# Taking weight signs from ScalarE to VectorE and a magnitude from VectorE to ScalarE, under a new set of order ranks

## The chip, the core and the metric

The kernel runs on one core of a Trainium2 chip. Its time is the device time of that core in microseconds (us), as the median of three runs. The engines are TensorE (PE, matmuls; its weight loads run beside them as PEld), VectorE (DVE), ScalarE (ACT), GpSimd (POOL), and the DMA queue that SyncE (SP) issues.

## What is computed

Three stages follow each other, with 4 x 576 = 2304 tokens of width 512 between them:

```python
scores = where(mask_local or mask_strided, q @ k.T / 8, -1e9)   # 4 batches, 8 heads, 576 tokens, 64 wide
x = softmax(scores) @ v                                         # 2304 x 512
h = x @ w_in;  g = maximum(0.01 * h, h);  x = g @ w_out         # layer 1, 512 -> 2048 -> 512
h = x @ w_in;  g = maximum(h, 0) + log1p(exp(-abs(h)))          # layer 2, its own weights
return g @ w_out
```

The four weight matrices arrive as 64-bit floats, the rest as 32-bit floats.

## The kernel before, in words

**Precision.** Every operand of the big products is split into two 16-bit floats, a high part and a rest, and a product is three matmuls (`mm3`, L461 to L464: high x high, high x rest, rest x high). `project` (L466) makes one block of h in 12 matmuls.

**Preparing a weight quarter.** A weight matrix is handled in four quarters of 2 MB (class `Weight`, from L140). `load` (L147) is a DMA on SP's queue. `largest` (L156, DVE) takes the biggest magnitude. `low` (L162, DVE) shifts the lower 32-bit word of each 64-bit number right by 29. `scale` (from L166, small DVE instructions) makes a scaling factor from the largest, after a matmul on PE (L122) has spread it over all partitions. `shift` (L209, ACT) multiplies the upper words, read as 32-bit floats, by that factor. `merge` (L214, DVE) shifts the upper word left by 3 and ORs the lower word in, which makes a 32-bit float; the left shift loses the sign, so the sign has to stand in the top bit of the lower word before that. There are two ways to put it there:

- `sign` (L198, DVE): takes the top 16 bits of the upper word AND 0x8000 and writes them into the top 16 bits of the lower word. It needs only the loaded word. Layer 2's two matrices use it.
- `sign_of_scaled` (L205, ACT): copies the scaled upper word as a 16-bit float into the same place; what is left of so small a number is its sign. It needs `shift` first. Layer 1's two matrices use it.

Then `high` (L221, ACT) and `rest` (L226, on POOL for layer 1's first matrix, on DVE for layer 2's first) or `rest_of` (L230, DVE) make the two 16-bit parts. `plan_quarter` (L730 on) plans this for layer 1's w_in (W1, four separate quarters) and layer 2's w_in (W2); `plan_together` (L695 on) plans layer 1's w_out (O1), all four quarters under one common scale. The chains are: W1 and O1: load, largest and low, scale, shift, sign of scaled, merge, high, rest. The areas that O1 is loaded into are those that W1's quarters leave, so each of O1's loads waits for a rest of W1.

**Stages.** First the attention of batches 0 and 1 runs beside the preparation of W1 and O1. Layer 1 is cut into eight units of 288 tokens: eight steps of `gate1` (PE, then L483 and L486 on ACT, L489 on POOL) and 16 blocks of the second product. Batches 2 and 3 and the preparation of layer 2's weights run beside layer 1. Layer 2 is cut into nine units of 256 tokens with eight steps each, 72 in all.

**A step of layer 2** (class `Unit`): `first` (PE, 24 matmuls into one of two h buffers in PSUM); `size` (L1136, DVE) clears the sign bits of h and writes |h| to SBUF; `relu` (L1143, ACT) writes max(h, 0) scaled, and frees the h buffer; `soft` (L1150 and L1151, ACT) makes ln(1 + exp(-scale x |h|)); `add` (L1155, POOL); `sums` (L1163, four DVE instructions); `cut_high` (L1167, ACT); `cut_rest` (L1171, DVE); `second` (PE, 21 matmuls). The results of `relu` have two places, and the place of step k is freed by `cut_rest` of step k for step k + 2.

**What sets the order.** Every operation is given to a `Plan` with an engine, a cost in us, what it depends on and a rank. `Plan.run` (L551 on) plays the schedule through in the costs given and issues the operations in that order: of those on an engine that could start within 0.5 us of the earliest, the one with the lowest rank is issued first. `RANKS` (L40) gives each kind of operation a start value and a slope. Engines run their instructions in the order issued. While PE would wait in the first 130 us of this schedule, dummy matmuls (L92) are put in. The plan books `sign_of_scaled` at 1.9 us, `sign` at 2.35 and `size` at 0.6.

Of the kernel before, what the change touches and what calls it, by code (L numbers as in the profile page):

```python
# [10 lines left out]
F16 = mybir.dt.float16  # L11
F32 = mybir.dt.float32
I32 = mybir.dt.int32
U32 = mybir.dt.uint32
U16 = mybir.dt.uint16
AF = mybir.ActivationFunctionType
ALU = mybir.AluOpType
# [4 lines left out]
B, H, S, D = 4, 8, 576, 64  # L22
# [17 lines left out]
RANKS = {  # L40
# [10 lines left out]
}  # L51
# [4 lines left out]
def build(tc, qt, kl, ks, v, wi1, wo1, wi2, wo2, mloc, mstr, out):  # L56
    nc = tc.nc
    with ExitStack() as ctx:
# [82 lines left out]
        class Weight:  # L141
# [54 lines left out]
            def sign(self, q):  # L196
# [3 lines left out]
                )  # L200

            def sign_of_scaled(self, q):

                w = self.t[q].bitcast(F16).rearrange("p s (n t) -> p s n t", t=4)
                nc.scalar.activation(w[:, :, :, 1], self.words(q)[1].bitcast(F32), AF.Copy)  # L205

# [380 lines left out]
        W1, O1, W2, O2 = Weight("i1", wi1), Weight("o1", wo1), Weight("i2", wi2), Weight("o2", wo2)  # L587
# [26 lines left out]
        plan = Plan({"mm": 2, "sc": 1, "pt": 1, "po": 1, "s": 4, "a": 3, "t": 3, "qk": 5, "rs": 2, "x2": 2, "gr": RING, "ob": 2}, idle, 130.0)  # L614
# [85 lines left out]
        def plan_together(W, name, after, parts, then, w1):  # L700
# [6 lines left out]
            for q in range(4):  # L707
                ld = plan.add("SP", 5.9, lambda q=q: W.load(q, area(q)), after[q], ("L" + name, q))
                big = step("DVE", 2.2, lambda q=q: W.largest(q, m()[:, q : q + 1]), [ld], q)
                low = step("DVE", 1.14, lambda q=q: W.low(q), [ld], q + 0.1, port=True)  # L710
                loads.append(big)
                read.append([big, low])

# [14 lines left out]
            for q in range(4):  # L728
                y = step("ACT", 2.07, lambda q=q: W.shift(q, st["s"]), [t] + read[q], 4 + q)
                y = step("ACT", 1.9, lambda q=q: W.sign_of_scaled(q), [y], 4 + q)  # L730
                y = step("DVE", 2.2, lambda q=q: W.merge(q), [y], 4 + q, port=True)
                y = step("ACT", 1.85, lambda q=q: W.high(q, parts(q), O1.by[:, q : q + 1]), [y] + made[-1:] * (q % 2), 4 + q)
                made.append(
                    step("DVE", 2.3, lambda q=q: W.rest_of(q, O1.by[:, q : q + 1]), [y], 4 + q, port=True)
                )
            return made, scaled

        def plan_quarter(W, name, q, place, after, parts, after_read, then=None, eng="DVE"):
# [21 lines left out]
            y = step("DVE", 1.14, lambda: W.low(q), [ld], 0.1, port=True)  # L760
            if not then:
                y = step("DVE", 2.35, lambda: W.sign(q), [y], 0.2, port=True)
            y = step("ACT", 2.07, lambda: W.shift(q, st["s"]), [sc, x, y], 0.3)
            if then:
                y = step("ACT", 1.9, lambda: W.sign_of_scaled(q), [y], 0.3)
            y = step("DVE", 2.2, lambda: W.merge(q), [y], 0.4, port=True)
# [131 lines left out]
        A, A1 = at[0], at[1]  # L898
# [174 lines left out]
        class Unit:  # L1073
# [34 lines left out]
            def scales(self):  # L1108
                new = lambda n, t: sml.tile([P, n], F32, name=t, tag=t)
                self.sc, self.nsc = new(4, "x2s"), new(4, "x2n")  # L1110
                nc.vector.tensor_scalar(
                    out=self.sc, in0=late["u2"], scalar1=self.p2, scalar2=2.0 ** -14, op0=ALU.mult, op1=ALU.mult
                )
                nc.vector.tensor_scalar(out=self.nsc, in0=self.sc, scalar1=-1.0, scalar2=None, op0=ALU.mult)

# [18 lines left out]
            def size(self, k):  # L1134
                t = self.a[k] = tmp.tile([P, 2, U1], F32, name="t", tag="t")[:, :, :U2]
                nc.vector.tensor_scalar(  # L1136
                    out=t.bitcast(I32), in0=self.ps[k].bitcast(I32), scalar1=0x7FFFFFFF, scalar2=None, op0=ALU.bitwise_and
                )

# [8 lines left out]
            def soft(self, k):  # L1148
                a = self.a[k]
                nc.scalar.activation(a, a, AF.Exp, scale=self.nsc[:, k // 2 : k // 2 + 1])  # L1150
                nc.scalar.activation(a, a, AF.Ln, bias=1.0)  # L1151
# [75 lines left out]
        for u in range(NU2):  # L1227
# [9 lines left out]
            for k in range(NK):  # L1237
# [4 lines left out]
                )  # L1242
                size = plan.add("DVE", 0.6, bind(U.size), [g1], rank("Fd", k), take=["t"])
                relu = plan.add(
# [95 lines left out]
```

## Time and profile before

| what | value |
|---|---|
| median of three runs | 870.89 us (870.03 to 873.74) |
| the profiled execution's own time | 871.47 us |
| its span | 869.5 us |
| mean granted TensorE clock in it | 0.995 |
| PE busy, of the span | 831.9 us, 96% |
| DVE busy | 533.7 us, 61% |
| ACT busy | 528.3 us, 61% |
| POOL busy | 265.0 us, 30% |

The shares are averages over stages with different limits. A busy PE says that matmuls were in the engine, dummy ones among them, and not that it was at its peak. The table by stretches (below) tells the stages apart.

### The profile page before, as it was taken

What the parts mean: (1) busy time and instruction counts of PE and PEld (TensorE: products, weight loads), DVE (VectorE), ACT (ScalarE), POOL (GpSimd) and SP (SyncE); (2) the same over time, 40 slices, a digit from 0 to 9 for tenths busy, and PEclk for the clock granted to TensorE, in tenths of its full rate; (3) what the DMA queues carried; (4) which work ended last, traced back from release to release, by engine and by line L of the source; (5) the groups of instructions that cost most, each with busy time, mean ns of one, the idle gap of its engine ahead of it and who ended that gap; (6) DMA issues with size and microseconds to landing.
All of it is one profiled execution on the core that took longest, in us unless ns stands there. A gap on an engine that the chain in (4) does not pass through costs nothing.

```text
span 869.5 us, 17639 instructions
## 1 busy us (share of the span) xinstructions
PE 831.9 (96%) x7330; PEld 684.6 (79%) x7330; DVE 533.7 (61%) x1232; ACT 528.3 (61%) x938; POOL 265.0 (30%) x194
## 2 busy tenths in 40 slices
PE   9888798799999999999999999999999999999997
PEld 5556576578777777787777777888888888888886
DVE  4895652542033535049647859977787778677684
ACT  5899979933456542263726457757575666657572
POOL 2365753120332124140504124323222322223131
PEclk9999999999999999999999999999999999999999
DMA  8932320121013470013221120000000000000000
GB/s 329 390 126 112 140 98 1 67 81 56 1 58 138 158 304 25 2 41 154 98 97 29 71 98 1 26 2 25 2 25 2 25 2 26 1 26 1 26 25 25
DMA packets 10991, 63.27 MB, mean 73 GB/s; under 512 B 1344, under 2 KB 1440, under 8 KB 7840
## 3 DMA queue, kind: packets, MB, share of 16 engines
q1 hardware_dynamic: 10656, 62.00, 19.0%
q8 instruction: 57, 0.93, 0.4%
q10 hardware_dynamic: 256, 0.16, 0.1%
q14 instruction: 22, 0.18, 0.1%
HBM read 57.44 MB, written 4.72 MB: 71 GB/s over the span
## 4 chain that ended last, share of the span: by engine, by line
PE 69%; ACT 12%; DVE 11%; DMA 3%; issue 3%; POOL 1%; SPq 0%; DVEq 0%; ACTq 0%; POOLq 0%
PE h L462 11%; PE h L464 11%; PE h L463 11%; PE o L462 10%; PE o L464 10%; PE o L463 10%; ACT pair L205 3%; ACT pair L209 2%; DMA pair<-wo_dram 2%; ACT s L368 2%; PE ps L322 2%; DVE pair L1005 2%; PE po L419 2%; PE pt L399 1%; ACT t L483 1%
## 5 line engine op out<-in xcount | busy, mean ns | idle before, releaser
L462 PE MATMUL h<-x,w 128*128 128x256 f16 (+1 forms) x1088 | 303.5, 279 | 7.2 <-ACT t L483 5.0
L464 PE MATMUL h<-x,w 128*128 128x256 f16 (+1 forms) x1088 | 303.4, 279 | 4.3 <-POOL w L226 4.3
L463 PE MATMUL h<-x,w 128*128 128x256 f16 (+1 forms) x1088 | 303.4, 279 | 0.0
L1155 POOL TENSOR_TENSOR pair<-pair,t 128x512 f32<-128x512 f32 x72 | 100.4, 1394 | 268.6 <-ACT t L1151 171.1
L489 POOL TENSOR_TENSOR g<-t,g 128x576 f16<-128x576 f32 x64 | 104.3, 1633 | 183.7 <-ACT g L486 181.7
L462 PE MATMUL o<-g,pair 128*128 128x288 f16 x512 | 147.7, 288 | 2.8 <-ACT pair L221 1.8
L464 PE MATMUL o<-g,pair 128*128 128x288 f16 x512 | 147.6, 288 | 2.5 <-DVE pair L230 2.5
L463 PE MATMUL o<-g,pair 128*128 128x288 f16 x512 | 147.5, 288 | 0.0
L463 PEld LDWEIGHTS <-w 128*128 128x128 f16 x1088 | 106.5, 98 | 27.3 <-issue 8.7
L464 PEld LDWEIGHTS <-w 128*128 128x128 f16 x1088 | 106.4, 98 | 24.3 <-POOL w L226 5.2
L462 PEld LDWEIGHTS <-w 128*128 128x128 f16 x1088 | 106.4, 98 | 19.4 <-issue 0.2
L1167 ACT ACTIVATE gr<-pair,x2b 128x896 f16<-128x896 f32 x72 | 74.0, 1038 | 57.2 <-DVE pair L1163 57.2
L1171 DVE SCALAR_TENSOR_TENSOR gr<-pair,x2b,gr 128x896 f16<-128x896 f32 x72 | 86.4, 1209 | 24.8 <-ACT gr L1167 24.7
L1163 DVE TENSOR_TENSOR pair<-pair 128x128 f32<-128x128 f32 x288 | 80.2, 324 | 16.8 <-POOL pair L1155 14.3
L1143 ACT ACTIVATE pair<-h,x2s 128x512 f32<-128x512 f32 x72 | 49.0, 680 | 60.0 <-DVE t L1136 54.4
L464 PE MATMUL o<-w,gr 128*128 128x256 f16 x306 | 83.4, 273 | 0.9 <-DVE gr L1171 0.7
L462 PE MATMUL o<-w,gr 128*128 128x256 f16 x306 | 83.4, 273 | 0.0
L463 PE MATMUL o<-w,gr 128*128 128x256 f16 x306 | 83.4, 273 | 0.0
L390 POOL TENSOR_TENSOR s<-s,sm 96x512 f32<-96x512 f32 (+3 forms) x48 | 43.7, 931 | 121.4 <-DVE sm L385 64.1
L483 ACT ACTIVATE t<-h,gs 128x576 f32<-128x576 f32 x64 | 47.0, 735 | 49.0 <-PE h L464 48.8
L1136 DVE TENSOR_SCALAR t<-h 128x512 int32<-128x512 int32 x72 | 48.7, 685 | 29.0 <-PE h L464 28.4
L214 DVE SCALAR_TENSOR_TENSOR pair<-pair 128x2048 int32<-128x2048 int32 x16 | 37.4, 2338 | 45.9 <-ACT pair L205 35.3
(123 smaller groups left out, 1391.1 us busy)
## 6 DMA issues: line engine op xcount, KB each, us to landing
pair<-wo_dram SPq DMA_DIRECT2D x12, 2048.0 KB, 7.8
pair<-wi_dram SPq DMA_DIRECT2D x8, 2048.0 KB, 10.1
out_dram<-pair SPq DMA_DIRECT2D x18, 256.0 KB, 2.2
q<-qt_dram SPq DMA_DIRECT2D x12, 288.0 KB, 5.9
v<-v_dram SPq DMA_DIRECT2D x2, 1408.0 KB, 7.7
pair<-v_dram SPq DMA_DIRECT2D x2, 1408.0 KB, 6.0
k<-ks_dram SPq DMA_DIRECT2D x7, 288.0 KB, 3.3
k<-kl_dram SPq DMA_DIRECT2D x5, 304.0 KB, 3.8
```

Of the source, the lines that this page charges most:

```text
L390: nc.gpsimd.tensor_tensor(out=sv, in0=sv, in1=rs, op=ALU.mult)
L462: nc.tensor.matmul(ps, ah, bh, start=first, stop=False)
L463: nc.tensor.matmul(ps, ah, bl, start=False, stop=False)
L464: nc.tensor.matmul(ps, al, bh, start=False, stop=last)
L483: nc.scalar.activation(t, ps, AF.Prelu, scale=gates[f // 4], alpha=0.01)
L489: nc.gpsimd.tensor_tensor(out=g[:, 1, f : f + 2, :], in0=t, in1=g[:, 0, f : f + 2, :], op=ALU.subtract)
L1136: nc.vector.tensor_scalar(out=t.bitcast(I32), in0=self.ps[k].bitcast(I32), scalar1=0x7FFFFFFF, scalar2=None, op0=ALU.bitwise_and)
L1143: nc.scalar.activation(r[:, :4].rearrange("p (j h) n -> p j (h n)", j=2), self.ps[k], AF.Relu, scale=self.sc[:, k // 2 : k // 2 + 1],)
L1155: nc.gpsimd.tensor_tensor(out=r, in0=r, in1=self.a[k], op=ALU.add)
L1163: nc.vector.tensor_tensor(out=r[:, o], in0=r[:, x], in1=r[:, y], op=op)
L1167: nc.scalar.activation(self.a[k][:, 0], self.r[k][:, 1:], AF.Copy, scale=self.ag)
L1171: nc.vector.scalar_tensor_tensor(out=a[:, 1], in0=self.r[k][:, 1:], scalar=self.ag, in1=a[:, 0], op0=ALU.mult, op1=ALU.subtract)
```

## The change

Layer 1's weights take their sign with `sign` on DVE, ahead of `shift`; `sign_of_scaled` is gone. For O1's fourth quarter the sign is ranked behind the common scale's first step. `size` becomes one ACT instruction, Prelu with slope -1 below zero and the scale of the column block, which gives the scaled magnitude; it now also waits for the unit's scales; Exp takes the constant -1 as its scale; the small DVE instruction that negated the scales is gone. All values of `RANKS` are new (36 pairs; the first rows and some others are shown).

```diff
-    "A0": (904.756, 0.733), "A1": (1181.967, 5.007), "A2": (1400.517, 32.745), "A3": (-265.753, 0.202),
-    "B0": (380.721, 6.480), "B1": (387.831, 20.804), "B2": (1471.672, 0.086), "B3": (530.207, 2.562),
...
-    "Fp": (-127.497, 0.075), "G0": (-198.498, 0.175), "G1": (1158.664, 0.271), "G2": (688.143, 68.364),
...
-    "O2l": (1380.929, 1.863), "S": (1139.158, 120.000), "S0": (1133.607, 120.000), "S1": (1442.075, 3.830),
-    "S2": (1500.000, 39.240), "W1m": (975.007, 5.818), "W1r": (1347.663, 2.158), "W2": (753.358, 37.166),
+    "A0": (840.876, 58.763), "A1": (1228.229, 40.415), "A2": (1416.066, 23.406), "A3": (497.717, 1.948),
+    "B0": (986.082, 6.642), "B1": (23.082, 0.143), "B2": (-175.176, 0.166), "B3": (496.207, 3.176),
...
+    "Fp": (-256.548, 21.319), "G0": (127.840, 0.080), "G1": (938.559, 22.340), "G2": (1155.015, 12.177),
...
+    "O2l": (1245.704, 0.744), "S": (867.671, 120.000), "S0": (882.390, 0.657), "S1": (1330.594, 0.312),
+    "S2": (1391.819, 36.045), "W1m": (350.471, 14.309), "W1r": (1476.384, 24.622), "W2": (-240.922, 1.069),
...
-            def sign_of_scaled(self, q):
-
-                w = self.t[q].bitcast(F16).rearrange("p s (n t) -> p s n t", t=4)
-                nc.scalar.activation(w[:, :, :, 1], self.words(q)[1].bitcast(F32), AF.Copy)
...
                 low = step("DVE", 1.14, lambda q=q: W.low(q), [ld], q + 0.1, port=True)
+                sign = step("DVE", 2.35, lambda q=q: W.sign(q), [low], q + 0.2 + 0.86 * (q == 3), port=True)
                 loads.append(big)
-                read.append([big, low])
+                read.append([big, sign])
...
                 y = step("ACT", 2.07, lambda q=q: W.shift(q, st["s"]), [t] + read[q], 4 + q)
-                y = step("ACT", 1.9, lambda q=q: W.sign_of_scaled(q), [y], 4 + q)
...
-            if not then:
-                y = step("DVE", 2.35, lambda: W.sign(q), [y], 0.2, port=True)
+            y = step("DVE", 2.35, lambda: W.sign(q), [y], 0.2, port=True)
             y = step("ACT", 2.07, lambda: W.shift(q, st["s"]), [sc, x, y], 0.3)
-            if then:
-                y = step("ACT", 1.9, lambda: W.sign_of_scaled(q), [y], 0.3)
...
-                self.sc, self.nsc = new(4, "x2s"), new(4, "x2n")
+                self.sc = new(4, "x2s")
...
-                nc.vector.tensor_scalar(out=self.nsc, in0=self.sc, scalar1=-1.0, scalar2=None, op0=ALU.mult)
...
-                nc.vector.tensor_scalar(
-                    out=t.bitcast(I32), in0=self.ps[k].bitcast(I32), scalar1=0x7FFFFFFF, scalar2=None, op0=ALU.bitwise_and
-                )
+                nc.scalar.activation(t, self.ps[k], AF.Prelu, scale=self.sc[:, k // 2 : k // 2 + 1], alpha=-1.0)
...
-                nc.scalar.activation(a, a, AF.Exp, scale=self.nsc[:, k // 2 : k // 2 + 1])
+                nc.scalar.activation(a, a, AF.Exp, scale=-1.0)
...
-                size = plan.add("DVE", 0.6, bind(U.size), [g1], rank("Fd", k), take=["t"])
+                size = plan.add("ACT", 0.6, bind(U.size), [g1, scaled], rank("Fa", k), take=["t"])
```

## Rows read from the trace of the kernel before

**Rows 1.** Busy time by stretch: stretch, length, PE, PEld, DVE, ACT, POOL, PEclk, DMA share, GB/s
```profile
22.00:51.00 29.00, 24.23 (x211) 15.02 (x210) 24.69 (x72) 24.74 (x78) 8.71 (x9) 1.00 0.73 301
51.00:130.00 79.00, 67.62 (x613) 52.41 (x612) 51.70 (x157) 70.79 (x137) 52.92 (x32) 1.00 0.35 127
130.00:172.00 42.00, 34.25 (x280) 26.25 (x277) 17.54 (x26) 40.29 (x35) 10.34 (x6) 0.99 0.10 35
172.00:178.00 6.00, 5.38 (x24) 3.44 (x25) 5.97 (x5) 6.00 (x22) 0.00 (x0) 0.52 0.00 0
178.00:500.00 322.00, 320.54 (x2779) 255.59 (x2777) 147.25 (x341) 149.00 (x309) 87.88 (x66) 1.00 0.24 89
500.00:560.00 60.00, 56.05 (x501) 48.43 (x500) 49.62 (x81) 37.95 (x50) 19.92 (x11) 1.00 0.10 38
560.00:862.00 302.00, 302.00 (x2768) 270.83 (x2767) 223.41 (x526) 187.70 (x260) 80.45 (x62) 1.00 0.04 15
```

**Rows 2.** The same view for the dummy matmuls of L92 alone, PE
```profile
22.00:51.00 29.00, 10.27 (x43) 1.00 0.73 301
51.00:180.00 129.00, 1.15 (x3) 0.97 0.26 92
```

**Rows 3.** Groups by line, ACT: busy us, mean ns of one, idle before and releaser
```profile
L205 ACT ACTIVATE pair<-pair 128x2048 f16<-128x2048 f32 x8 | 38.3, 4784 | 0.1
L1143 ACT ACTIVATE pair<-h,x2s 128x512 f32<-128x512 f32 x72 | 49.0, 680 | 60.0 <-DVE t L1136 54.4 <-DVE gr L1171 4.7
L483 ACT ACTIVATE t<-h,gs 128x576 f32<-128x576 f32 x64 | 47.0, 735 | 49.0 <-PE h L464 48.8 <-POOL s L390 0.2
L78 ACT ACT_TABLE_LOAD x1 | 1.3, 1283 | 0.7 <-PEq L1330 0.7
```

**Rows 4.** Timelines of ACT, DVE, POOL and PE: W1's first quarter up to its first product
```profile
39.88 4.77 ACT L205 ACTIVATE pair<-pair 128x2048 f16<-128x2048 f32 x1
44.68 2.29 DVE L214 SCALAR_TENSOR_TENSOR pair<-pair 128x2048 int32<-128x2048 int32 x1 [2.90 <-ACT pair L205]
49.09 4.08 POOL L226 TENSOR_TENSOR w<-pair,w 128x2048 f16<-128x2048 f32 x1 [10.13 <-ACT w L221]
53.22 0.30 PE L464 MATMUL h<-x,w 128*128 128x288 f16 x1 [1.54 <-POOL w L226]
```

**Rows 5.** The chain that ended last, at the end of O1's preparation: start, us
```profile
163.19 4.80 ACT pair L205
168.01 2.29 DVE pair L214
...
172.62 0.42 PE o L464
```

**Rows 6.** Groups by line, DVE, and line L198 alone (ns min/median/max, first and last start)
```profile
L1136 DVE TENSOR_SCALAR t<-h 128x512 int32<-128x512 int32 x72 | 48.7, 685 | 29.0 <-PE h L464 28.4
...
L198 DVE TENSOR_SCALAR pair<-pair x8: 2458/2466/3441, 328.9 to 520.0; 128x2048 uint16<-128x2048 uint16 x8
```

**Rows 7.** Timeline of DVE: the first merge of O1, and DVE's idle time before it
```profile
138.88 2.29 DVE L214 SCALAR_TENSOR_TENSOR pair<-pair 128x2048 int32<-128x2048 int32 x1 [8.72 <-ACT pair L205]
```

**Rows 8.** Timelines of POOL and DVE: an add alone, and one begun beside a sign
```profile
513.68 1.27 POOL L1155 TENSOR_TENSOR pair<-pair,t 128x512 f32<-128x512 f32 x1 [3.75 <-ACT t L1151]
520.01 3.44 POOL L1155 TENSOR_TENSOR pair<-pair,t 128x512 f32<-128x512 f32 x1 [1.99 <-ACT pair L1143]
520.00 2.47 DVE L198 TENSOR_SCALAR pair<-pair 128x2048 uint16<-128x2048 uint16 x1
```

**Rows 9.** Timelines of ACT and DVE: one turn of relu's two places in layer 2
```profile
665.05 0.69 ACT L1143 ACTIVATE pair<-h,x2s 128x512 f32<-128x512 f32 x1 [6.29 <-DVE t L1136]
670.58 1.28 DVE L1171 SCALAR_TENSOR_TENSOR gr<-pair,x2b,gr 128x896 f16<-128x896 f32 x1 [0.39 <-ACT gr L1167]
671.96 0.69 ACT L1143 ACTIVATE pair<-h,x2s 128x512 f32<-128x512 f32 x1
```

10 rows, old and new, of the table RANKS are left out of this document.

## The prediction

> **What bounds the kernel now.** I read the busy time by stretch first, because the averages of the page mix stages. From 178 us on PE has work nearly without a gap: 320.5 of 322 us, then all of 302 us from 560 to 862 [rows 1]. There the other engines are covered, and time can be won only where PE stands still. It stands still in two places. One is the front. Between 51 and 130 us PE is idle for 11.4 us (79 less 67.6), between 130 and 172 for 7.8, and between 172 and 178 for 0.6. In that last stretch the granted clock is 0.52, the lower of its two levels (1.2 GHz of 2.4), after 42 us with the 7.8 us of gaps: 24 matmuls took 5.38 us, 0.224 each, where one takes 320.5 / 2779 = 0.115 later on. That is 2.6 us more [rows 1]. Dummy matmuls hide another 10.3 us of waiting from 22 to 51 us, and 1.2 after [rows 2]. The other place is the start of layer 2, 500 to 560 us: PE idle for 3.95 us, while DVE is busy for 49.6 of 60 [rows 1].
>
> Who holds PE up in the front is seen in the ACT column: 70.8 of 79 us, then 40.3 of 42, then 6.0 of 6 [rows 1]. Second I read the groups of ACT. The sign of the scaled word costs 4.78 us an instruction, eight times, 38.3 us in all [rows 3]; the plan that fixed the order books it at 1.9. Third I followed it along the chains. In W1's first quarter it runs from 39.9 to 44.7, DVE's merge waits for it, then come the high part, POOL's rest and PE's first full product at 53.2 [rows 4]. At the end of O1 the chain of waits goes sign, merge, rest, product: 163.2 to 172.6 us [rows 5]. DVE meanwhile sits idle for 8.7 us before a single merge [rows 7] and is busy for only 17.5 of 42 us [rows 1]. So the front is an ACT queue with the signs in it.
>
> **Part 1: eight signs leave ACT and go to DVE.** ACT loses 8 x 4.78 = 38.3 us [rows 3], one sign (4.8) before 51 us, three (14.4) to 130, four (19.1) after. DVE gains 8 x 2.47 = 19.8 us [rows 6]. The new sign needs only the loaded word, so it can run while the largest goes through PE and becomes a scale; what waits for it is `shift` on ACT, and behind that whatever ACT has next, attention's copies and exponentials in the front. All gains are capped by what PE loses, since PE's own work doesn't shrink.
>
> Start. The first product waits for the end of a chain that loses 4.77 us [rows 4]. If DVE does the new sign wholly ahead of `shift`, all of it is gained; if it delays `shift` by its own length, 4.77 - 2.47 = 2.3 is left. DVE is busy for 24.7 of 29 us there [rows 1], so I take a value between: 3.3 us.
>
> 51 to 130 us. Of the 11.4 us idle and 1.2 of dummies, 1.5 is the wait at 53.2 already counted [rows 4]; that leaves 11. ACT would fall from 70.8 to 56.4 of 79. The bounds are 0 (DVE, 51.7 of 79, or POOL takes over) and 11. Three W1 chains lose 4.8 us each on ACT, and ACT was what PE's feed stood behind, but PE's feed also passes POOL, 52.9 of 79. I take 6 us.
>
> 130 to 178 us. The loss is 7.8 + 0.6 + 2.6 = 11 us. ACT sheds 19.1 of 46.3 busy us, and O1's signs fall into DVE's idle time; O1's fourth load is the only one whose sign can stand next to the scale, one sign of 2.47 at most. The bounds are 0 and 11. I take 9: what follows is one chain of shift, merge, high and rest for four quarters, with ACT at about 65%, and without the gaps the clock has no cause to fall.
>
> A W1 quarter that is finished earlier also frees its area earlier, so O1's loads on SP's queue are issued earlier, as are batch 2's v loads behind them; nothing is moved past them in that queue.
>
> The signs bring a price on POOL. An add that takes 1.27 us alone took 3.44 when it began 0.01 us after a sign on DVE [rows 8]: it stood for 2.2 us until the sign was over. POOL does W1's rest, which PE waited for [rows 4]. From both sides: nothing, if no sign meets a POOL instruction on PE's path, or one meeting for each of W1's quarters, 4 x 2.2 = 8.8 us. I took 6 and not more in the middle term for this; it contains about 2 us of such meetings. The Trainium skill, "SBUF — State Buffer", section "Who interferes with whom", says that a port pair shared by VectorE and GpSimd is locked for a whole instruction, and that ScalarE never waits on anyone; by that rule a sign on ScalarE is free of this and one on VectorE is not. The row agrees. With a meeting for every quarter the sum below would be about 7 us smaller.
>
> **Part 2: `size` leaves DVE for ACT.** DVE loses 72 x 0.685 us [rows 6]. The new instruction's nearest rows are the Relu of the same shape from the same PSUM buffer with the same kind of scale, 0.680, and layer 1's Prelu, 0.735 for 576 columns where this has 512 [rows 3]. So ACT gains 72 x 0.68 = 49 us. The table is loaded once in the whole run, and Prelu and Exp both run after it [rows 3], so no load is added. From 560 to 862 us ACT would go from 187.7 to about 230 of 302 us (62 of the 72 steps lie there) [rows 1]; PE's work covers it, and I cost it at nothing. If that cover went, it would be rival C. The added wait for the unit's scales ends before the unit's first h is complete, since the scales follow x's rest by a few small instructions and 24 matmuls follow it too. Behind `size` on ACT stand only the same step's instructions and the cuts of earlier ones. The negation that disappears is one small DVE instruction per unit, covered too.
>
> 500 to 560 us. DVE is what PE waits for, and it sheds one `size` per step, about nine, 9 x 0.6 = 5.4 us of issue. Bounds 0 and 3.95; I take 2.5, since the last quarter's parts of layer 2's w_out are still due there.
>
> **Part 3: ranks.** They reorder whatever is ready within 0.5 us. W1's second half (W1m) moves ahead of attention's first batch on ACT (350 against 841 and 986), which helps the start. I cost the rest at 0, with 4 us either way.
>
> **The sum.** 3.3 + 6 + 9 + 2.5 = 20.8 us off the profiled execution's 871.47 us gives 850.7. The median of the runs shown, 870.89, is 0.6 lower, so 850.
>
> **Rivals.**
>
> A, **DVE and the shared port become the front's bound.** For it: DVE is already at 24.7 of 29 us before 51 [rows 1], and the port row [rows 8]. Against it: DVE's idle time in O1's stage [rows 7]. Then the start gives 2.3, the middle nothing, O1's stage 7 and layer 2's start 1.5, 10.8 us together: 860. Chance 0.18.
>
> B, **the front takes nearly the whole ceiling.** 4.8 + 11 + 11 + 4 = 30.8 us: 840. It needs two engines (ACT at 56 of 79, POOL at 53) to feed PE without a gap in order. Chance 0.08.
>
> C, **slower, through relu's two places.** From a relu to the second one after it the row shows 6.9 us [rows 9], and PE needs 2 x 45 x 302 / 2768 = 9.8 us for two steps [rows 1], so 2.9 are spare. With `size` on ACT, four instructions of the next step (2.7 us) can stand ahead of a cut, and another `size` (0.6) ahead of the relu: 10.2, over by 0.4 per two steps. It decides from 0.6 on, where 36 pairs eat the 21 us; with one more instruction in the way, 0.9, it costs 32 and the time is 882. Against it: the order is laid out with ACT booked close to its true cost, and today's turn has no such pile. Chance 0.06.
>
> D, **the signs were covered anyway**: the front hangs on loads and on the attention, and the time stays at 868 to 872. Against it is the chain [rows 5]. Chance 0.06.
>
> The forecast has 0.62. A measurement of this kernel can tell about 0.5%, 4.4 us, from no change. Forecast, A and B are faster by more than that: 0.88. D is within it, 0.06, and C slower, 0.06. The range runs from 841, nearly all of B, to 863, A with its ranks 3 us worse; C, D and the outer tails are left out.
>
> **What would show it.** Right: no L205; sixteen signs of about 2.5 us on DVE; ACT below 60 of 79 us from 51 to 130; the first full product near 50 us; O1's last rest some 20 us earlier than 178; no stretch at the lower clock there; PE without a gap in layer 2 with ACT near 76%. Wrong: PE idle in the front as much as now with DVE or POOL as releaser (A); relus that wait for `cut_rest` and gaps before `first` after 560 us (C); a first product still at 53 (D).

## The result, and the profile after

The changed kernel takes 864.81 us (median of 7 executions, 861.92 to 869.53), the one before 872.74 in the same measurement (870.03 to 874.45). The ratio is 0.9913 [0.9888, 0.9938]: 7.9 us faster, where 20.8 were forecast. The direction holds, the size does not, and 864.8 lies 2 us above the range. The profiled execution took 867.42 us, 4.05 less than the profiled one of before, so what its trace shows has to add up to 4, not to 7.9.

Busy time by stretch after the change (length, PE, PEld, DVE, ACT, POOL, granted clock, DMA share, GB/s), to be laid beside [rows 1]:

```profile
22.00:51.00 29.00, 23.62 (x211) 14.80 (x213) 27.77 (x78) 22.59 (x89) 14.29 (x10) 0.99 0.68 270
51.00:130.00 79.00, 75.02 (x639) 55.50 (x640) 67.64 (x176) 57.89 (x148) 53.83 (x32) 0.96 0.34 128
130.00:172.00 42.00, 39.84 (x316) 31.29 (x315) 33.63 (x17) 24.13 (x25) 17.30 (x8) 0.96 0.22 77
172.00:178.00 6.00, 6.00 (x59) 4.77 (x58) 2.52 (x9) 3.31 (x7) 1.28 (x1) 1.00 0.01 3
178.00:500.00 322.00, 317.90 (x2744) 253.34 (x2743) 141.96 (x328) 146.56 (x304) 88.02 (x63) 1.00 0.24 87
500.00:560.00 60.00, 57.30 (x518) 50.07 (x516) 42.93 (x72) 47.76 (x67) 18.56 (x12) 1.00 0.07 26
560.00:700.00 140.00, 140.00 (x1284) 125.58 (x1283) 91.78 (x225) 100.79 (x149) 37.66 (x29) 1.00 0.04 13
700.00:858.00 158.00, 158.00 (x1450) 141.68 (x1449) 94.69 (x228) 113.39 (x167) 42.05 (x32) 1.00 0.04 15
```

By the PE column the front has gained: 75.0 of 79 us are busy where 67.6 were, so 7.4 us of idleness are gone. The column misleads. Two more views say what PE was busy with. First the dummy matmuls alone, for [rows 2]:

```profile
51.00:180.00 129.00, 8.39 (x32) 3.09 (x32) 0.96 0.28 103
```

There are 8.4 us of dummies after 51 us, where 1.2 were; they hide 7.2 us of waiting from the PE column. Second, the granted clock in short stretches shows three where PE ran at the lower level (1.2 GHz) for a part of the time. In each PE had stood still just before: 2.65 us ahead of 50.80, 1.20 ahead of 112.29 and 2.16 ahead of 142.80. Before the change there was one such stretch, at 172:

```profile
50.00:55.00 5.00, 4.20 (x24) 2.67 (x25) 2.61 (x22) 1.65 (x8) 4.07 (x4) 0.66 0.89 311
110.00:115.00 5.00, 3.15 (x18) 2.01 (x17) 4.92 (x23) 4.44 (x8) 2.92 (x1) 0.71 0.00 0
142.00:147.00 5.00, 4.20 (x21) 2.81 (x22) 5.00 (x4) 3.15 (x3) 1.88 (x1) 0.66 0.01 3
```

What counts is the number of real products done. The same view for one tile alone gives them: in each fence below the first two lines are tile h (first product of a unit) and the last is tile o (second product), with PE's instruction count behind its busy time. From 500 to 560 us all of PE's matmuls are products, so the tables by stretch have their number there. Before the change:

```profile
51.00:130.00 79.00, 53.65 (x412) 0.00 (x0) 11.96 (x17) 1.00 0.35 127
130.00:178.00 48.00, 21.09 (x166) 0.00 (x0) 4.53 (x7) 0.93 0.09 31
...
130.00:178.00 48.00, 17.88 (x122) 0.00 (x0) 0.00 (x0) 0.93 0.09 31
```

After it:

```profile
51.00:130.00 79.00, 50.45 (x381) 11.06 (x15) 0.96 0.34 128
130.00:178.00 48.00, 19.01 (x149) 4.43 (x6) 0.96 0.19 67
...
130.00:178.00 48.00, 25.69 (x192) 0.00 (x0) 1.67 (x4) 0.96 0.19 67
```

At 0.115 us for a product (320.54 / 2779 in [rows 1]) this is an account of the change by stretch. To 130 us: 381 against 412, **31 fewer, 3.6 us lost**. From 130 to 178: 149 + 192 = 341 against 288, 53 more, 6.1 us won. From 500 to 560: 518 against 501, 17 more, 2.0 us won. The sum is 4.5, near the 4.05 between the two profiled executions.

Products are not all of PE's work, though. What is left of PE's counts without products and dummies are attention's matmuls and those that spread a maximum. Of these the changed kernel has done 12 fewer before 51 us, 28 more from 51 to 130 (226 against 198), 16 more from 130 to 178, and 32 fewer from 178 to 500. In that last stretch it makes as many products as before (2350 and 2353) with PE busy for 2.64 us less, which prices one of the others at 0.07 us (an estimate). With them the account reads: 0.9 us lost before 51, 1.6 lost to 130, 7.3 won to 178, 2.6 lost to 500, 2.0 won to 560; 4.2 in all. Most of the loss against the forecast sits before 130 us, and 2.6 us of it in layer 1's stretch, which the prediction put at nothing.

The chain of waits shows what the front hangs on now (start, us, instruction; a part is left out):

```profile
98.32 1.09 DVE pair L162
...
100.41 2.96 DVE pair L198
103.40 2.20 ACT pair L204
105.62 4.44 DVE pair L209
110.09 1.91 ACT w L216
...
113.27 0.35 PE h L457
```

Sign (L198) and merge (L209) of a W1 quarter stand in it one behind the other with ACT's shift (L204) between them, and the merge takes 4.4 us where it takes 2.29 alone [rows 4]. GpSimd's timeline says why:

```profile
98.49 5.70 POOL L385 TENSOR_TENSOR s<-s,sm 108x432 f32<-108x432 f32 x4 [1.15 <-DVE sm L380]
104.15 3.76 POOL L484 TENSOR_TENSOR g<-t,g 128x576 f16<-128x576 f32 x3
```

The merge that began at 105.62 ended at 110.06, 2.15 us after POOL's three adds did (104.15 + 3.76 = 107.91), about its own length. The groups by line from 22 to 190 us show it on average, where an undisturbed sign takes 2.43 us and an undisturbed merge 2.29 (busy us, mean ns):

```profile
L198 DVE TENSOR_SCALAR pair<-pair 128x2048 uint16<-128x2048 uint16 x8 | 23.1, 2888 | 0.0
L209 DVE SCALAR_TENSOR_TENSOR pair<-pair 128x2048 int32<-128x2048 int32 x8 | 21.4, 2689 | 3.2 <-ACT pair L204 3.2
```

The merges waited 35.3 us for ACT's sign in the same view of the kernel before; 3.2 us are left. That wait went as predicted; in the chain above, sign and merge on DVE stand in its place.

### The profile page after: what moved, and what is told of

It is laid out like the page before. It is cut to its first block, busy times and chain, and to the rows that moved or that the text cites. A ratio compares the mean times of both kernels' runs of the same rounds, so it can differ in the third digit from the quotient of the medians.

```text
span 865.6 us, 17668 instructions
## 1 busy us (share of the span) xinstructions
PE 839.2 (97%) x7356; PEld 689.0 (80%) x7356; DVE 518.9 (60%) x1159; ACT 528.2 (61%) x1002; POOL 277.7 (32%) x194
## 4 chain that ended last, share of the span: by engine, by line
PE 66%; DVE 17%; DMA 8%; ACT 5%; issue 2%; POOL 1%; DVEq 0%; POOLq 0%; ACTq 0%
PE o L457 10%; PE o L459 10%; PE o L458 10%; PE h L457 10%; PE h L459 10%; PE h L458 10%; DMA pair<-wo_dram 6%; DVE pair L198 3%; DVE m L156 2%; DVE pair L209 2%; DMA pair<-wi_dram 2%; PE ps L317 2%; ACT pair L204 1%; DVE pair L162 1%; DVE pair L997 1%
## 5 line engine op out<-in xcount | busy, mean ns | idle before, releaser
L1144 POOL TENSOR_TENSOR pair<-pair,t 128x512 f32<-128x512 f32 x72 | 98.3, 1369 | 268.7 <-ACT pair L1132 140.5
L1160 DVE SCALAR_TENSOR_TENSOR gr<-pair,x2b,gr 128x896 f16<-128x896 f32 x72 | 88.4, 1231 | 63.7 <-ACT gr L1156 63.6
L385 POOL TENSOR_TENSOR s<-s,sm 96x512 f32<-96x512 f32 (+3 forms) x48 | 58.3, 1235 | 69.2 <-DVE sm L380 34.8
L1127 ACT ACTIVATE t<-h,x2s 128x512 f32<-128x512 f32 x72 | 48.7, 677 | 43.1 <-PE h L459 42.9
L832 ACT ACTIVATE x<-o,xs 128x576 f32<-128x576 f32 (+1 forms) x18 | 12.0, 684 | 90.6 <-PE o L459 90.6
L459 PEld LDWEIGHTS <-pair 128*128 128x128 f16 x512 | 50.3, 98 | 16.3 <-DVE pair L225 2.5
```

The lines of the kernel that those rows point to most:

```text
L385: nc.gpsimd.tensor_tensor(out=sv, in0=sv, in1=rs, op=ALU.mult)
L459: nc.tensor.matmul(ps, al, bh, start=False, stop=last)
L1127: nc.scalar.activation(t, self.ps[k], AF.Prelu, scale=self.sc[:, k // 2 : k // 2 + 1], alpha=-1.0)
L1144: nc.gpsimd.tensor_tensor(out=r, in0=r, in1=self.a[k], op=ALU.add)
L1160: nc.vector.scalar_tensor_tensor(out=a[:, 1], in0=self.r[k][:, 1:], scalar=self.ag, in1=a[:, 0], op0=ALU.mult, op1=ALU.subtract)
```

## The experiments

The theory to be tested, D: ScalarE's relief is real, and the vector engine's signs give most of it back, through its queue and the port that it shares with GpSimd. The rivals: R, the new ranks hold W1's rests up; O, the new order as a whole is the loss and the signs are nearly free. The letters D, R and O in the expectations stand for these (the prediction has a rival D of its own, which is another).

### Parts of the change under either set of ranks

Four kernels, each planned anew by the kernel's own planner. The changed kernel with the ranks of before:

```diff
-    "A0": (840.876, 58.763), "A1": (1228.229, 40.415), "A2": (1416.066, 23.406), "A3": (497.717, 1.948),
+    "A0": (904.756, 0.733), "A1": (1181.967, 5.007), "A2": (1400.517, 32.745), "A3": (-265.753, 0.202),
...
```

> The whole change, but with the ranks of before. Theory R (the new ranks read O1's first quarters ahead of W1's on VectorE and so keep W1's rests as late as before): 850 to 858 us, with W1's four rests on GpSimd starting earlier than the 45, 73, 93 and 112 us of the changed kernel. Theory D (VectorE and the port it shares with GpSimd are full in the front, whatever the order): 862 to 868 us, rests as late as in the changed kernel.

Measured: 915.04 us, ratio 1.0477 [1.045, 1.0505]. The kernel before with the new ranks (the same lines the other way round):

> The kernel before with the new ranks only. Theory R: slower than before, 876 to 885 us, since the ranks delay W1. Theory D: the ranks are neutral, 868 to 874 us.

Measured: 902.44 us, 1.0349 [1.0318, 1.038]. The signs alone, with the ranks of before:

```diff
-            if not then:
-                y = step("DVE", 2.35, lambda: W.sign(q), [y], 0.2, port=True)
+            y = step("DVE", 2.35, lambda: W.sign(q), [y], 0.2, port=True)
...
-                y = step("ACT", 1.9, lambda q=q: W.sign_of_scaled(q), [y], 4 + q)
```

> Only the signs go to VectorE; the magnitude stays there and the ranks are those of before. Theory R: 852 to 860 us. Theory D: 864 to 870 us, with PE waiting on VectorE or GpSimd in the front. If the gain comes from the magnitude's move instead: 869 to 873 us.

Measured: 910.99 us, 1.0439 [1.0415, 1.0463]. The magnitude alone, with the ranks of before:

```diff
-                size = plan.add("DVE", 0.6, bind(U.size), [g1], rank("Fd", k), take=["t"])
+                size = plan.add("ACT", 0.6, bind(U.size), [g1, scaled], rank("Fa", k), take=["t"])
```

> Only the magnitude goes to ScalarE; the signs stay there and the ranks are those of before. Theories R and D: 868 to 873 us, as at most the 4 us of PE's idle time from 500 to 560 us can be won. If relu's two places bind (rival C): 876 us or more, with idle PE after 560 us.

Measured: 876.59 us, 1.0044 [1.0023, 1.0064]. The time is that of rival C, but its other mark is missing: PE is idle for 0.2 us after 560. The loss lies at layer 2's start, with PE busy for 55.12 of 60 us from 500 to 560 at a granted clock of 0.97.

What follows: the first three lie outside every range stated, so these runs do not choose between D and R. Each set of ranks fits its own set of operations. The change with the old ranks is 50 us over the change, the new ranks without the change 29 us over the kernel before, the signs with the old ranks 37. A kernel planned anew therefore measures an order more than a part. The third kernel still shows a mechanism. The timeline of POOL and DVE in it:

```profile
110.35 2.03 POOL L385 TENSOR_TENSOR s<-s,sm 108x216 f32<-108x216 f32 x2
111.50 9.65 DVE L198 TENSOR_SCALAR pair<-pair 128x2048 uint16<-128x2048 uint16 x1
112.34 4.06 POOL L221 TENSOR_TENSOR w<-pair,w 128x2048 f16<-128x2048 f32 x1
116.36 2.51 POOL L484 TENSOR_TENSOR g<-t,g 128x576 f16<-128x576 f32 x2
```

A sign of 2.47 us took 9.65: it began while POOL was at work, POOL went on without a gap until 118.87, and the sign ended 2.3 us later. Everything behind it in DVE's queue stood as long.

### The signs left out, in either order

To see a part without a new plan, the instructions alone were taken out, and the order was kept. The kernel before without L205:

```diff
             def sign_of_scaled(self, q):
-                w = self.t[q].bitcast(F16).rearrange("p s (n t) -> p s n t", t=4)
-                nc.scalar.activation(w[:, :, :, 1], self.words(q)[1].bitcast(F32), AF.Copy)
+                pass
```

> The kernel before with its order and without the eight sign instructions of layer 1's weights on ScalarE (layer 1 is then computed with the weights' magnitudes). It prices the first half of the change alone: ScalarE's relief with nothing put on VectorE. If the prediction's terms for the front were right on that side: 851 to 857 us. If the order as issued, laid out with the signs booked at 1.9 us, holds PE up by itself: 862 us or more.

Measured: 853.96 us, 0.9779 [0.9761, 0.9797]. The changed kernel without layer 1's signs on DVE:

```diff
             def sign(self, q):
+                if self.name in ("i1", "o1"):
+                    return
```

> The changed kernel with its order and without the eight sign instructions of layer 1's weights on VectorE (layer 1 with magnitudes). It prices the second half. Theory D (the signs on VectorE and their meetings with GpSimd gave back what ScalarE's relief won): 850 to 858 us. Theory O (the order, with its dummy matmuls and PE's place in its own queue, is what is left; the signs are covered): 861 to 865 us.

Measured: 856.95 us, 0.9818 [0.9798, 0.9838].

These two split the result. ScalarE's relief in the order of before: 872.79 (the kernel before in this measurement) - 853.96 = 18.8 us. From there to the changed kernel without signs, which adds the new order and the magnitude: 3.0 us slower. With the eight signs on DVE: 864.81 - 856.95 = 7.9 us slower. -18.8 + 3.0 + 7.9 = -7.9. D's part is the larger of the two losses. O's is there as well, and it is more than 3.0. Layer 2's relu shows where each part falls (first and last start in us, behind the lengths in ns; the kernel before, without ACT's signs, the new order without signs, the change):

```profile
L1143 ACT ACTIVATE pair<-h,x2s x72: 665/687/692, 506.6 to 850.5; 128x512 f32<-128x512 f32 x72
L1142 ACT ACTIVATE pair<-h,x2s x72: 666/687/694, 488.9 to 832.7; 128x512 f32<-128x512 f32 x72
L1134 ACT ACTIVATE pair<-h,x2s x72: 667/672/687, 494.2 to 835.9; 128x512 f32<-128x512 f32 x72
L1132 ACT ACTIVATE pair<-h,x2s x72: 667/671/692, 504.0 to 845.9; 128x512 f32<-128x512 f32 x72
```

ScalarE's relief brings layer 2 forward by 17.7 us, the new order puts it back by 5.3 and the signs by 9.8 (the profiled execution of the change is 2.6 us slower than its median). Layer 2 itself, from the first relu to the last, is 2.0 us shorter in the change than before (341.9 against 343.9), with its own new order and the magnitude on ACT. So the 3.0 are a loss of 5.3 ahead of layer 2 and a gain of about 2 in it.

Products by tile in the first of the two (two lines of h, one of o):

```profile
51.00:130.00 79.00, 60.30 (x460) 0.00 (x0) 13.69 (x19) 0.98 0.33 123
130.00:178.00 48.00, 14.55 (x117) 0.00 (x0) 3.99 (x6) 1.00 0.19 68
...
130.00:178.00 48.00, 31.93 (x258) 0.00 (x0) 1.68 (x4) 1.00 0.19 68
```

and in the second:

```profile
51.00:130.00 79.00, 54.44 (x420) 12.51 (x17) 0.99 0.34 126
130.00:178.00 48.00, 20.11 (x158) 5.11 (x7) 1.00 0.26 92
...
130.00:178.00 48.00, 24.80 (x200) 0.00 (x0) 1.68 (x4) 1.00 0.26 92
```

To 130 us: 412 products before, 460 with ACT's signs left out (5.5 us), 420 in the new order without signs, 381 with them. From 130 to 178: 288, then 375 (10.0 us), 358 and 341. In products alone the order takes 57 by 178 us (6.6 us) and the signs 56 (6.4). But the new order has PE do more of the other matmuls in this time: from 51 to 178 us they are 214 without ACT's signs, 288 in the new order without signs, and 258 with them. At 0.07 us each the order has 5 of its 6.6 us back by 178, and the signs lose 2 more. The order's loss comes mostly after that, in layer 1's stretch: PE is idle for 4.2 us of 312 (178 to 490), where it was for 1.2 of 307 (178 to 485).

The order also holds W1's later rests up, as R has it: without any sign the third and fourth start at 91.27 and 107.33 us, against 85.47 and 100.16 in the order of before. What that alone costs no run shows.

### The magnitude put back, and W1's rank

The changed kernel with `size` on DVE again, under the new ranks:

```diff
-                size = plan.add("ACT", 0.6, bind(U.size), [g1, scaled], rank("Fa", k), take=["t"])
+                size = plan.add("DVE", 0.6, bind(U.size), [g1], rank("Fd", k), take=["t"])
```

> The changed kernel, new ranks, with the magnitude back on VectorE as before. The front is laid out as in the changed kernel, so the difference is the magnitude's move: 866 to 869 us if it wins the 2.5 us of the prediction, 863 to 866 if it wins nothing, below 862 if it costs.

Measured: 873.71 us, 0.9997 [0.9981, 1.0013]: 8.9 us more than the change, and outside all three ranges. This kernel too was planned anew. The loss lies at layer 2's start, where PE stands still and its clock falls:

```profile
500.00:520.00 20.00, 16.97 (x139) 14.27 (x138) 16.27 (x22) 11.59 (x14) 5.52 (x3) 0.91 0.10 43
520.00:540.00 20.00, 16.70 (x137) 13.79 (x136) 15.84 (x28) 14.42 (x21) 5.55 (x4) 0.91 0.00 1
```

PE's waits there are for the relu and the cuts. In the changed kernel the same two stretches have PE busy for 18.43 and 19.61 us at the full clock. Layer 2 takes 347.9 us from the first relu to the last, 4.0 more than in the kernel before, so the 8.9 are what `size` on DVE costs in this order, not in general. Theory R was tried by giving W1's reading a rank ahead of w_out's:

```diff
-"W1r": (1476.384, 24.622)
+"W1r": (1090.000, 2.000)
```

> The changed kernel with one rank changed, so that VectorE reads W1's quarters (largest, low, sign) ahead of O1's. Theory R: 852 to 860 us, with W1's second to fourth rest on GpSimd starting before 72, 93 and 112 us. Theory D: 862 to 870 us, the rests no earlier.

Measured: 920.21 us, 1.0538 [1.052, 1.0557], outside both ranges. W1's second to fourth rest did come earlier, at 53.96, 64.01 and 78.36 us, and yet layer 1's first product came at 99.1: PE's longest wait from 22 to 190 us (us in total, times, longest) is for one of attention's spreads on POOL.

```profile
PE pt L394 <- POOL s L385: 30.5, 2, 28.6
```

So earlier rests are not enough. Whether R holds beyond this stays open, since the whole plan moved with the one rank.

### The signs on DVE in the order of before

Here nothing is planned anew. The order of before stays on every engine; ACT's sign is left out as above, and DVE makes it in its own queue directly behind `low`:

```diff
             def low(self, q):
...
+                if self.name in ("i1", "o1"):
+                    self.sign(q)
```

> The kernel before with its own order of instructions on every engine; only each of layer 1's eight ScalarE signs is left out and the vector engine makes it in that place of its own queue where it has just written the part's low words. Floor: 854 us, what the kernel before takes without ScalarE's signs. Theory D (the vector engine and the port that it shares with GpSimd carry the price of the signs): 8 us over the floor as in the change's order, so 858 to 866 us, and up to 874 if all eight of 2.47 us stand on the chain. Rival O (the signs are nearly free on the vector engine, and the change's loss is its new order of instructions): 854 to 857 us.

Measured: 871.79 us, 0.9994 [0.9982, 1.0006]. All but 1 us of the relief is given back: 17.8 us over the floor of 854. The same two lines ahead of `merge` instead:

> As the run with the signs behind the low words, but the vector engine makes each sign directly ahead of the part's merge, which comes after ScalarE's shift. Theory D: the sign now delays the merge and what follows it by its own 2.5 to 4.6 us, where the other place delays the low words' readers: 856 to 870 us, within 5 us of the other place. Rival O: 854 to 857 us.

Measured: 865.86 us, 0.9922 [0.9909, 0.9935]: 12 over the floor. O falls as the main cause: in the order of before the signs on DVE cost more than in the new one. The place costs 6 us. Both parts of the change in the order of before (the first of the two places, and `size` as ACT's Prelu where DVE had it):

> The run with the signs behind the low words, and with layer 2's magnitude made by ScalarE in the vector engine's place of the order (both halves of the change, the order of the kernel before kept). The magnitude alone cost 3.9 us in the order of before and was worth 8.9 us in the change's own. If what it is worth hangs on the order: 0 to 4 us slower than the run without it. If it is worth something whenever the signs have left ScalarE: 3 to 9 us faster than that run.

Measured: 873.71 us, 1.0017 [1.0006, 1.0028], 1.9 slower than without the magnitude's move. Only w_out's four signs on DVE, behind `low`:

```diff
-                if self.name in ("i1", "o1"):
+                if self.name == "o1":
                     self.sign(q)
```

> Only the four signs of w_out's layer 1 go to the vector engine, behind the low words; those of W1 stay on ScalarE, where they were. Four signs of 4.78 us leave ScalarE, so if its relief counts where w_out is split as much as where W1 is, half of the 18.8 us: 862 to 866 us. If nearly all of the relief lies in W1's stretch (51 to 130 us) the run stands at 868 to 873 us; if it lies in w_out's, where the vector engine has room, at 854 to 859 us.

Measured: 870.81 us, 0.9965 [0.9945, 0.9984]. That lies in the range for a relief that falls into W1's stretch. But the range took the signs on DVE as free, and they have a price here too (four of 4.14 us on average), so the run does not tell the cases apart.

### The engine's time or the port

What is it in a sign that costs so much, its time on DVE or the port? A maximum over the same words has nearly a sign's length (2.28 against 2.43 us), and it was not lengthened in any trace. It was put in the two places in the sign's stead:

```diff
                 if self.name in ("i1", "o1"):
-                    self.sign(q)
+                    x = sml.tile([P, 1], F32, name="x", tag="wx")
+                    nc.vector.tensor_reduce(
+                        out=x, in_=self.words(q)[1].bitcast(F32), axis=AX.XY, op=ALU.max, apply_absolute_value=True
+                    )
```

> The run with the signs behind the low words (871.8 us, 17.8 over the floor of 854), but each of the eight signs is replaced by a maximum over the same words (2.28 us, against 2.43 for an undisturbed sign), which stood at 2.28 us in every trace so far, beside GpSimd or not; layer 1 is computed with its weights' magnitudes. If the signs' price is the vector engine's own time in that place of its queue: 868 to 872 us. If it is the port that the sign shares with GpSimd: 855 to 861 us. In between, both.

Measured: 862.71 us, 0.9879 [0.9862, 0.9895].

> The same replacement in the other place, ahead of the merges (865.9 us with signs, 12 over the floor); layer 1 is computed with its weights' magnitudes. Engine's own time: 863 to 866 us. Port: 855 to 859 us.

Measured: 862.52 us, 0.9868 [0.985, 0.9887].

Both times lie in between, so both causes are there. Eight instructions of this length on DVE cost 8.8 and 8.6 us over the floor, nearly the same in either place: that is DVE's own time, in its queue and in the chain that waits for it. A sign in the same place costs 9.1 us more behind `low` and 3.3 more ahead of `merge`; 8 x 0.15 = 1.2 of each is its greater length, and the rest goes with what the sign does and the maximum doesn't. By the ratios, which take out the difference between the measurements, the 9.1 and 3.3 are 10.0 and 4.7. The groups from 22 to 190 us show it. Signs behind `low` (DVE's sign, POOL's spread, POOL's rest):

```profile
L200 DVE TENSOR_SCALAR pair<-pair 128x2048 uint16<-128x2048 uint16 x8 | 24.7, 3084 | 0.3
...
L391 POOL TENSOR_TENSOR s<-s,sm 96x512 f32<-96x512 f32 (+3 forms) x24 | 28.5, 1210 | 40.0 <-ACT s L369 19.0 <-DVE sm L386 9.7 <-DVE sm L381 8.8
L227 POOL TENSOR_TENSOR w<-pair,w 128x2048 f16<-128x2048 f32 x4 | 18.2, 4548 | 21.1 <-ACT w L222 21.1
```

Maxima in the same place:

```profile
L167 DVE TENSOR_REDUCE x<-pair 128x1 f32<-128x2048 f32 x8 | 18.2, 2272 | 0.0
...
L394 POOL TENSOR_TENSOR s<-s,sm 96x512 f32<-96x512 f32 (+3 forms) x24 | 23.3, 993 | 38.5 <-ACT s L372 19.0 <-DVE sm L384 8.5 <-DVE sm L389 4.8
L230 POOL TENSOR_TENSOR w<-pair,w 128x2048 f16<-128x2048 f32 x4 | 16.3, 4076 | 17.6 <-ACT w L225 17.6
```

Beside the signs POOL's spreads are 5.2 us longer and its rests 1.9, and the signs are 24.7 - 8 x 2.43 = 5.3 us longer than alone; the maxima stay at 2.27. The Trainium skill, "SBUF — State Buffer", section "Who interferes with whom", says which instructions take the pair shared with GpSimd: a `tensor_scalar` can, a `tensor_reduce` on trn2 never does. Both rows agree with it.

### A division between the engines

In the order of the change, the signs of parts 1 and 3 on ACT behind its shift, the others on DVE:

```diff
             def sign(self, q):
+                if self.name in ("i1", "o1") and q % 2:
+                    return
...
             def shift(self, q, s):
...
+                if self.name in ("i1", "o1") and q % 2:
+                    w = self.t[q].bitcast(F16).rearrange("p s (n t) -> p s n t", t=4)
+                    nc.scalar.activation(w[:, :, :, 1], hi.bitcast(F32), AF.Copy)
```

> The change with its own order, but the signs of parts 1 and 3 of W1 and of w_out's layer 1 are made by ScalarE behind its shift, as in the kernel before; parts 0 and 2 stay on the vector engine. Four signs of 4.78 us go back to ScalarE, which is busy for 58 of 79 us there, and four of 2.9 us leave the vector engine, busy for 68. The signs cost 7.9 us on the vector engine in this order. If its load is the bound and ScalarE has room: half of that comes back, 859 to 863 us. If both engines' places in the order matter, as in the runs so far: 865 to 880 us.

Measured: 875.97 us, 1.0028 [1.0012, 1.0044]. The same with `self.name == "o1"` for the condition, w_out's signs on ACT:

> The change with its own order, but w_out's four layer 1 signs are made by ScalarE behind its shift; W1's four stay on the vector engine. From 130 to 172 us the vector engine is busy for 34 of 42 us and ScalarE for 24. If the vector engine's load is the bound to the end of the front: 859 to 863 us. If ScalarE's longer sign delays the last merges that layer 1's products wait for: 866 to 874 us.

Measured: 876.28 us, 1.0031 [1.0017, 1.0045], 2 us above the second range. Four signs moved back cost 11 us each time, more than all eight cost on DVE. In the second, the kernel's busy time by stretch has ACT at 39.86 of 42 us from 130 to 172 and PE at 33.45, nearly the picture of [rows 1], though at a granted clock of 0.84: w_out's shift, sign, merge and high follow one another there, and a longer sign on ACT lengthens that chain. (This is argued from the busy times; no run separates it.) No version measured that makes all its signs beats the change; the sign ahead of `merge` in the order of before comes to the same time as the change (865.86 and 864.81, with intervals of the ratio that overlap).

## Why the prediction was wrong in size

**What bounds the kernel: right.** The front is an ACT queue with the signs in it. Without ACT's signs, and with all else kept, the kernel takes 18.8 us less. The three terms for the front add up to 18.3 (3.3 + 6 + 9), which is what the relief brings with nothing put on DVE, though a price for the signs there was said to be in them. That price is 7.9 us, and the new order, put at 0, costs about 5 ahead of layer 2. These are the two steps that failed.

**The start, 3.3 us: wrong, and the step is the ranks at nothing.** W1's first rest did start earlier on POOL, at 45.17 instead of 49.09 [rows 4], as much as the term asked for. PE used nothing of that. The timelines of POOL, DVE and PE:

```profile
45.17 4.46 POOL L221 TENSOR_TENSOR w<-pair,w 128x2048 f16<-128x2048 f32 x1 [6.46 <-ACT w L216]
46.90 2.76 DVE L371 TENSOR_SCALAR sm<-sm 96x8 f32<-96x8 f32 x1
50.80 1.17 PE L317 MATMUL ps<-k,q 64*96 64x128 f32 x8 [2.65 <-DVE mx L340]
...
52.76 2.32 PE L92 MATMUL idle<-idb 128*128 128x512 bf16 x7
54.91 0.49 PE L394 MATMUL pt<-ident,s 96*128 96x96 f32 x4
55.25 0.29 PE L457 MATMUL h<-x,w 128*128 128x288 f16 x1
```

The new order puts attention's scores, seven dummies and a transposition ahead of the first product, which comes at 55.25; the first with a rest stood at 53.22 [rows 4], and near 50 was forecast. The scores came late themselves. A small instruction of attention on DVE (L371, 0.16 us at the median) began while POOL made that rest and took 2.76 us, until the rest was over; PE waited 2.65 us for the maxima behind it. It took 2.77 us in the new order without signs as well, so this is not the signs' doing: the order brought the two engines together at a place where no sign is.

**51 to 130 us, 6 us: wrong, and the step is "it contains about 2 us of such meetings".** With the start the two terms were to bring 9.3 us, and in products they lost 3.6 (about 2.5 with the other matmuls counted). Of what ACT's relief brings there (5.5 us) the signs took 4.5; the order took 4.6 in products, about half of it for attention's matmuls done earlier. The prediction looked at what a sign does to POOL (an add that stood for 2.2 us) and not at what POOL does to a sign and to a merge on DVE, whose queue then stands. It also counted DVE's 19.8 us as filling idle time, when in the order of before even eight undisturbed instructions of that length cost 8.6 us.

**130 to 178 us, 9 us: right in kind, 6.1 measured in products, about 7.3 with the others.** The lower clock at 172 went, and so did most of the gaps. Relief alone brings 10.0 there; the order and the signs take 2.0 each in products.

**500 to 560 us, 2.5 us: 2.0 measured.** Twelve `size` instructions stood in this stretch before, with 8.10 us, and not nine of 0.6. `size` takes 0.677 us on ACT (0.68 forecast):

```profile
L1127 ACT ACTIVATE t<-h,x2s 128x512 f32<-128x512 f32 x72 | 48.7, 677 | 43.1 <-PE h L459 42.9
L1132 ACT ACTIVATE pair<-h,x2s 128x512 f32<-128x512 f32 x72 | 48.6, 674 | 6.9 <-DVE gr L1160 6.9
```

PE has no gap after 560 us, with ACT busy for (100.79 + 113.39) / 298 = 72%; 76% was forecast. What the move is worth hangs on the order: 8.9 us in the new one, and 2.7 (876.59 against 873.84) and 1.9 us lost in two with the ranks or the order of before.

**The ranks, 0 with 4 us either way: wrong.** Order and magnitude together are 3.0 us slower without any sign, the order alone about 5 ahead of layer 2, and a set of ranks beside the wrong operations cost 29 to 50. Two numbers of the trace belong to this term: 7.2 us more dummies, and layer 1's 322 us with 317.90 busy instead of 320.54.

**Rivals.** A came nearest, with 0.18 against the forecast's 0.62: DVE and the shared port did become the front's bound, its O1 term (7) and its start of layer 2 (1.5) fit the 6.1 and 2.0, and its 860 falls short of 864.8 because its start (2.3) did not come and the middle lost where A put nothing. B falls, and so does C: ACT's idle time before the relu, spent waiting for `cut_rest`, is 6.9 us over 72 steps, and after 560 us PE waits for nothing. The prediction's D (the signs were covered) falls with the 18.8 us.

**What was to show it.** No L205, sixteen signs of 2.5 us at the median, ACT at 57.9 of 79 and PE without a gap after 560 us came as written. O1's last rest came 16 us earlier (it began at 159.75 instead of 175.48), where some 20 were named. The first product did not come early, and the lower clock moved instead of going. "PE idle in the front as much as now", the sign given for A, did not show, since dummies filled PE: it had to be looked for in the products.

## What to carry to other kernels

An instruction moved to an engine with idle time still costs that engine's queue: here eight cost 8.6 us over the floor before any contention, and 12 to 18 with it (in the order of before), so price a move both for what it does to the neighbour on a shared port and for what the neighbour does to it and to all that is queued behind. Count the useful instructions by stretch, not the busy time, wherever a kernel can fill its waits with dummies. Test a part of a re-planned kernel in place, with the order kept, since a plan made anew changes more than the part does.

## What the hardware showed that was not expected

A DVE instruction that meets GpSimd can stand through several GpSimd instructions that follow back to back, not only through one: the sign of 9.65 us waited for a rest and two adds that had not begun when it started. It need not: the sign at 100.41 in the chain above was over after 2.96 us, while POOL's four spreads went on to 104.19. A small instruction can stand as long as a large one: one over 96 x 8 numbers took 2.76 us beside a rest, where the median of its kind is 0.16. What the meetings cost hangs on the place in the queue: with the same eight instructions, what the signs cost beyond the maxima was 9.1 us behind `low` and 3.3 ahead of `merge`.

A copy on ACT that writes 16-bit numbers 8 bytes apart takes 4.78 us for 2048 columns [rows 3], where the shift of the same words, with 32-bit results 8 bytes apart, takes 2.20 in the chain above.
